# Decode attention beside a feed-forward block: K turned as 32-bit pairs, with q and P as the stationary operands

## The chip, the cores and the metric

The kernel runs on one core of one Trainium2 chip. The metric is device time in microseconds (us). The kernel before takes 122.8 us (median of 3 runs, 122.71 to 122.98).

Engine names: PE is the matrix engine (TensorE), PEld its weight loads, DVE the vector engine, ACT the scalar engine, POOL is GpSimd, SP the engine that issues the loads. A "unit" below is one batch with four KV heads: 1 MB of K and 1 MB of V. There are 16 of them.

## The reference, cut to what matters

```python
# x: [8, 1, 512]; 32 query heads, 8 KV heads of width 128; the last 1024 of 4096 cached keys are used
xn = layernorm(x)
q  = xn @ wq                                   # [512, 4096]
s  = (softmax(q k^T / sqrt(128)) v) @ wo       # over k_cache, v_cache[:, :, -1024:, :]
g  = silu((gelu(xn @ w_gate) * (xn @ w_up)) @ w_down)
return x + s * g
```

Everything is bfloat16. The work reads 47.5 MB, of which K and V are 33.6 MB (32 loads of 1,024 KB, each called 1 MB here), and produces 8 KB. The term `s * g` is so small beside `x` that an experiment that leaves attention out still passes the comparison with the reference. That comparison therefore says nothing for the experiments below that are called wrong on purpose, and little for the others: where "right result" stands below, it means that this comparison was passed by a kernel that does the whole arithmetic.

## The kernel before

All large loads go through one queue, from SP, in a fixed order: `wq`, then K and V of unit after unit, then the feed-forward weights and `wo`. A ring of ten 2 MB buffers lets the loads run ahead. One unit of attention is:

```python
def transposes(u, t):                  # four times per unit, 8 chunks of 128 (head, key) rows each
    for i in range(TG):
        nc.tensor.transpose(kT_ps[:, i*P:(i+1)*P], k_t[b][:, h, t*TG+i, :], ident)
    nc.vector.tensor_copy(out=kT, in_=kT_ps)

def scores(u, t):                      # kT is stationary, 16 columns of q move
    for i in range(TG):
        nc.tensor.matmul(sc[u][:, t*TG+i, :], kTs[u, t][:, i*P:(i+1)*P],
                         qT[:, b, h*HS:(h+1)*HS], ...)
    # after the last: ACT Exp -> pT (already with keys on partitions)

def values(u):                         # V is stationary, 16 columns of P move
    nc.tensor.matmul(sum_ps, ones_pp, pT[u], ...)
    for c in range(NCH):               # 32
        nc.tensor.matmul(oT_ps, v_t[b][:, h, c, :], pT[u][:, c, :], ...)
    nc.vector.tensor_reduce(out=sums, in_=sum_ps..., op=ALU.add)
    nc.vector.reciprocal(out=sums, in_=sums)
    nc.vector.tensor_tensor(out=oT[:, h, :, b], in0=oT_ps, in1=sums, op=ALU.mult)
# ... the loop over units issues the loads of K[u] and V[u-1], and interleaves these three
```

The projection by `wo` already uses column tiles: four matmuls with 32 stationary columns each, in four strips of the array.

The softmax here doesn't subtract the row's maximum and nothing guards it: scores larger than these inputs give would overflow.

## Time and profile before

| | before |
|---|---|
| time | 122.8 us |
| loads | 47.5 MB, DMA engines full from 3 to 112 us |
| one unit of loads | every 4.9 us |
| PE's wait for K in a unit | about 0.9 us |
| last weight lands | 116.86 us |

These are lines of the page of the kernel before. The first block gives busy time, share of the span and instructions; the strips give tenths of 40 slices of the span (9 is 90% or more), the GB/s row what the loads moved; the queue lines give packets, MB and the share of the time of 16 DMA engines; then the chain of work that ended last; then the two costliest groups (instructions, shapes, busy us, mean ns, idle time before them and its cause).

```profile
span 121.0 us, 4362 instructions
PE 85.1 (70%) x2015; PEld 78.7 (65%) x2030; DVE 69.8 (58%) x145; ACT 13.3 (11%) x22; POOL 1.4 (1%) x6
...
PEclk9999999999976999999999999599999955555555
DMA  4999999999999999999999999999999999999720
...
q1 hardware_dynamic: 5976, 47.47, 93.6%
q8 instruction: 16, 0.26, 0.8%
...
DMA 95%; DVE 0%; PE 0%; SPq 0%; issue 0%
...
L200 DVE COPY kT<-kT_ps 128x1024 bf16<-128x1024 bf16 x64 | 43.0, 692 | 16.0 <-PE kT_ps L196 16.0
L196 PE MATMUL kT_ps<-ident,k_t 128*128 128x128 bf16 x512 | 41.9, 230 | 11.8 <-DMA k_t<-in_A_k_cache_dram 11.8
```

The DMA strip is 9 from the second slice to the 37th, and the chain is DMA for 95% of the span. PE is busy for 70%, and most of what it waits for is a load (11.8 us for K, 8.4 us for `wq` at the start), which is the sign of an engine that keeps up. A note for reading on: PE's busy time is a union of overlapping, pipelined matmuls. It is not the time that PE needs per unit. The 512 transposes have a mean of 230 ns, yet eight of them take 0.61 us.

The timeline of the kernel before around one K wait (start, duration, engine, instruction, idle time and releaser):

```profile
61.79 0.46 PEld L196 LDWEIGHTS <-k_t 128*128 128x128 bf16 x8
61.81 0.61 PE L196 MATMUL kT_ps<-ident,k_t 128*128 128x128 bf16 x8
...
63.48 0.62 PE L196 MATMUL kT_ps<-ident,k_t 128*128 128x128 bf16 x8 [0.87 <-DMA k_t<-in_A_k_cache_dram]
```

### The profile page before, as it was taken

Reading aid. Unit: us, or ns where it says so; the run is one execution under the profiler, and the core shown is the slowest. Engines: PE = TensorE matmul, PEld = TensorE weight load, DVE = VectorE, ACT = ScalarE, POOL = GpSimd, SP = SyncE. Lnnn points to the kernel's source line nnn. Section 1 sums busy time; section 2 is a strip of 40 time slices with the busy share of each in tenths; the row PEclk is TensorE's granted clock in tenths of the full one; section 3 lists DMA queues with packets and bytes.
Section 4 is the critical chain, followed back from the end, with each engine's and each line's share of the span. In section 5 each row is a group of like instructions: output and inputs, shape, how many; then the busy total and the mean of one; then the engine's idle time right before and its main releaser. Section 6 shows DMA issues by size and latency. Waiting matters only on the chain.

```text
span 121.0 us, 4362 instructions
## 1 busy us (share of the span) xinstructions
PE 85.1 (70%) x2015; PEld 78.7 (65%) x2030; DVE 69.8 (58%) x145; ACT 13.3 (11%) x22; POOL 1.4 (1%) x6
## 2 busy tenths in 40 slices
PE   0000699897879978879669693997969697845760
PEld 0000699896878977769669683896968597744640
DVE  3710036886947969669687592787859400398010
ACT  4500000110101101101101010110101100100000
POOL 4000000000000000000000000000000000000000
PEclk9999999999976999999999999599999955555555
DMA  4999999999999999999999999999999999999720
GB/s 100 423 433 433 401 420 420 433 423 431 417 428 423 420 431 415 428 423 428 423 420 417 431 425 428 428 423 420 417 449 433 418 419 440 438 417 409 316 88 3
DMA packets 6009, 47.75 MB, mean 395 GB/s; under 512 B 736, under 2 KB 744, under 8 KB 1000
## 3 DMA queue, kind: packets, MB, share of 16 engines
q1 hardware_dynamic: 5976, 47.47, 93.6%
q8 instruction: 16, 0.26, 0.8%
q10 hardware_dynamic: 16, 0.01, 0.0%
q14 instruction: 1, 0.01, 0.0%
HBM read 47.46 MB, written 0.01 MB: 392 GB/s over the span
## 4 chain that ended last, share of the span: by engine, by line
DMA 95%; DVE 0%; PE 0%; SPq 0%; issue 0%
DMA k_t<-in_A_k_cache_dram 51%; DMA wg_t<-in_B_w_gate_dram 18%; DMA wo_t<-in_A_wo_dram 17%; DMA wq_t<-in_A_wq_dram 10%; PE s_ps L355 0%; SPq L89 0%; DVE tmp L363 0%; DVE out_sb L365 0%; SPq L97 0%
## 5 line engine op out<-in xcount | busy, mean ns | idle before, releaser
L200 DVE COPY kT<-kT_ps 128x1024 bf16<-128x1024 bf16 x64 | 43.0, 692 | 16.0 <-PE kT_ps L196 16.0
L196 PE MATMUL kT_ps<-ident,k_t 128*128 128x128 bf16 x512 | 41.9, 230 | 11.8 <-DMA k_t<-in_A_k_cache_dram 11.8
L196 PEld LDWEIGHTS <-k_t 128*128 128x128 bf16 x512 | 31.8, 103 | 12.9 <-DMA k_t<-in_A_k_cache_dram 12.9
L213 PE MATMUL sc_ps<-qT,kT 128*128 128x16 bf16 x512 | 22.4, 170 | 0.5 <-DVE kT L200 0.4
L213 PEld LDWEIGHTS <-kT 128*128 128x128 bf16 x512 | 20.6, 98 | 2.9 <-issue 0.8
L220 ACT ACTIVATE pT<-sc_ps 128x512 bf16<-128x512 f32 x16 | 9.6, 597 | 80.8 <-PE sc_ps L213 80.8
L231 PEld LDWEIGHTS <-v_t 128*128 128x128 bf16 x512 | 15.5, 97 | 2.4 <-issue 0.8
L231 PE MATMUL oT_ps<-pT,v_t 128*128 128x16 bf16 x512 | 15.5, 170 | 1.3 <-issue 0.5
L235 DVE TENSOR_REDUCE sums<-sum_ps 128x16 f32<-128x512 f32 x16 | 11.0, 690 | 1.4 <-PE kT_ps L196 0.7
L178 PE MATMUL qT_ps<-xnT,wq_t 128*128 128x8 bf16 x128 | 3.7, 168 | 8.4 <-DMA wq_t<-in_A_wq_dram 8.4
L178 PEld LDWEIGHTS <-wq_t 128*128 128x128 bf16 x128 | 3.6, 104 | 8.5 <-DMA wq_t<-in_A_wq_dram 8.5
L207 PE MATMUL sc_ps<-mask,ident 128*128 128x512 bf16 x15 | 6.5, 430 | 0.0
L185 DVE CAST qT<-qT_ps 128x256 bf16<-128x256 f32 x1 | 0.4, 425 | 10.2 <-PE qT_ps L178 10.2
L355 PE MATMUL s_ps<-wo_t,oR 128*32 128x128 bf16 x128 | 4.2, 309 | 2.3 <-DMA wo_t<-in_A_wo_dram 2.3
L355 PEld LDWEIGHTS <-oR 128*32 128x32 bf16 x128 | 3.4, 139 | 2.9 <-issue 2.9
L290 DVE TENSOR_SCALAR z<-z 128x112 f32<-128x112 f32 x1 | 0.2, 219 | 8.4 <-ACT z L289 8.4
L239 DVE TENSOR_TENSOR oT<-oT_ps,sums 128x16 bf16<-128x16 f32 x16 | 3.7, 229 | 2.1 <-PE kT_ps L196 0.5
L238 DVE RECIPROCAL sums<-sums 128x16 f32<-128x16 f32 x16 | 4.0, 253 | 0.5
L279 PE MATMUL gu_ps<-xnT,wg_t 128*128 128x8 bf16 x56 | 3.5, 201 | 0.8 <-DMA wg_t<-in_B_w_gate_dram 0.8
L279 PE MATMUL gu_ps<-xnT,wu_t 128*128 128x8 bf16 x56 | 3.5, 202 | 0.7 <-DMA wu_t<-in_B_w_up_dram 0.7
L279 PEld LDWEIGHTS <-wg_t 128*128 128x128 bf16 x56 | 3.4, 161 | 0.9 <-DMA wg_t<-in_B_w_gate_dram 0.9
L279 PEld LDWEIGHTS <-wu_t 128*128 128x128 bf16 x56 | 3.5, 161 | 0.8 <-DMA wu_t<-in_B_w_up_dram 0.8
(51 smaller groups left out, 26.5 us busy)
## 6 DMA issues: line engine op xcount, KB each, us to landing
k_t<-in_A_k_cache_dram SPq DMA_DIRECT2D x16, 1024.0 KB, 20.5
v_t<-in_A_v_cache_dram SPq DMA_DIRECT2D x16, 1024.0 KB, 19.8
wq_t<-in_A_wq_dram SPq DMA_DIRECT2D x2, 2048.0 KB, 9.6
wo_t<-in_A_wo_dram SPq DMA_DIRECT2D x1, 2048.0 KB, 27.6
wg_t<-in_B_w_gate_dram SPq DMA_DIRECT2D x1, 1792.0 KB, 21.6
wu_t<-in_B_w_up_dram SPq DMA_DIRECT2D x1, 1792.0 KB
wd_t<-in_B_w_down_dram SPq DMA_DIRECT2D x1, 1792.0 KB, 25.2
wo_t<-in_A_wo_dram SPq DMA_DIRECT2D x1, 1024.0 KB, 27.4
```

The lines of the kernel that those rows point to most:

```text
L178: nc.tensor.matmul(qT_ps[:, h, :], wq_t[k // 2][:, k % 2, h * Dh : (h + 1) * Dh], xnT[:, k, :], start=(k == 0), stop=(k == KD - 1),)
L196: nc.tensor.transpose(kT_ps[:, i * P : (i + 1) * P], k_t[b][:, h, t * TG + i, :], ident)
L200: nc.vector.tensor_copy(out=kT, in_=kT_ps)
L207: nc.tensor.matmul(sc[u].rearrange("p c h -> p (c h)"), ident, mask.rearrange("p c n j -> p (c n j)"), start=True, stop=False, skip_group_ ...
L213: nc.tensor.matmul(sc[u][:, t * TG + i, :], kTs[u, t][:, i * P : (i + 1) * P], qT[:, b, h * HS : (h + 1) * HS], start=False, stop=(t == NT ...
L220: nc.scalar.activation(out=pT[u], in_=sc[u], func=ACT.Exp, scale=inv_sqrt_dh)
L231: nc.tensor.matmul(oT_ps, v_t[b][:, h, c, :], pT[u][:, c, :], start=(c == 0), stop=(c == NCH - 1))
L235: nc.vector.tensor_reduce(out=sums, in_=sum_ps.rearrange("p c h -> p h c"), axis=AX.X, op=ALU.add)
L238: nc.vector.reciprocal(out=sums, in_=sums)
L239: nc.vector.tensor_tensor(out=oT[:, h, :, b], in0=oT_ps, in1=sums, op=ALU.mult)
L279: nc.tensor.matmul(gu_ps[:, w, j, :], wt[:, k, :].rearrange("p (m j) -> p j m", j=FJ)[:, j, :], xnT[:, k, :], start=(k == 0), stop=(k == K ...
L355: nc.tensor.matmul(s_ps[32 * q : 32 * (q + 1), :], oR[:, t, i, :], w[:, r, q * NW : (q + 1) * NW], start=(t == 0 and i == 0), stop=(t == N ...
```

## The change

The intent is to give PE less to do. Two neighbouring keys of 128 bf16 values are read as 128 words of 32 bits, and one fp32 transpose turns both. Then q is the stationary operand for the scores, and P for V, each with 32 columns in four column tiles, so that long rows of K and V stream through the array. P must now be turned, and partial sums of V over strips and pairs must be gathered, with fp32 matmuls against a selecting matrix that add each unit into one bank per head half. The order of units changes from batch-major to head-half-major for that gather. The diff, cut to its core:

```diff
-        b, h = divmod(u, NH)
+        h, b = divmod(u, B)
 ...
-        for i in range(TG):
-            nc.tensor.transpose(kT_ps[:, i*P:(i+1)*P], k_t[b][:, h, t*TG+i, :], ident)
+        k32 = k_t[u // 2][:, u % 2, :, :].rearrange("p c d -> p (c d)").bitcast(FP32)
+        for pc in range(NPC):                                  # 4 per group, 16 per unit
+            w = g * NPC + pc
+            nc.tensor.transpose(kT_ps[:, pc, :], k32[:, w*P:(w+1)*P], identf)
 ...
-            nc.tensor.matmul(sc[u][:, t*TG+i, :], kTs[u, t][:, i*P:(i+1)*P], qT[...], ...)
+        for r in range(2):
+            for g in range(NG):
+                nc.tensor.matmul(sc_ps[CC*g:CC*(g+1), :], Q2[:, r, b, h, :, :]...,
+                                 kTs[u, g][:, :, r], ..., tile_position=(0, CC*g))
 ...
+    def turn(u):                                               # 4 bf16 transposes of P
+        ...
+        nc.scalar.copy(out=pTs[u], in_=pT_ps)
 ...
-            nc.tensor.matmul(oT_ps, v_t[b][:, h, c, :], pT[u][:, c, :], ...)
-        nc.vector.tensor_reduce(out=sums, ...); reciprocal; product
+                nc.tensor.matmul(x_ps[CC*g:CC*(g+1), :, :]..., pTs[u][:, pc, CC*g:CC*(g+1)],
+                                 v_t[u // 2][:, u % 2, c:c+2, :]..., tile_position=(0, CC*g))
+        nc.vector.tensor_tensor(out=xs[u][:, 0:2*Dh]..., in0=x_ps, in1=own2..., op=ALU.mult)
+    def gather(u):                                             # fp32, 257 columns
+        nc.tensor.matmul(tot[h], zsel[:, B-1-b:P+B-1-b], xs[u], start=(b == 0), stop=(b == B-1))
+    def outputs(t): ...                                        # normalise, expand: once per head half
```

No byte less is read, and the loads keep their sizes, their count and their places in the queue.

## The prediction

> **What bounds the kernel now.** The DMA stream. The page's chain of work that ended last is 95% DMA; the slices show the 16 DMA engines at "9" from 3 us to about 112 us at 415 to 433 GB/s, 47.5 MB in all. The Trainium skill, "DMA: Bandwidth & Descriptors", Specifications, gives 435 GB/s as the fabric ceiling; this trace's 424 GB/s is 97% of that. The queue's own waits show loads held by earlier loads, only 0.6 us by PE releasing a buffer. One unit (1 MB of K, 1 MB of V) arrives every 4.9 us. In it PE does about 4 us of work and waits about 1 us for K (timeline, 60 to 70 us). After the last weight lands at 116.86 us there are only 12 matmuls, two DVE operations and the output DMA.
>
> **What the change does, per unit.**
> - Loads: the same sizes and counts, heads and batches in another order.
> - PE removed: 32 bf16 transposes (8 take 0.61 us, so 2.4), 32 score matmuls (1.4), 32 V matmuls (0.95), the sums matmul (0.2).
> - PE added: 16 fp32 transposes; 8 score matmuls of 512 columns and 16 V matmuls of 256 in four column tiles; 4 bf16 transposes of P; one fp32 gather of 257 columns. The old projection already has column tiles: 64 of 128 columns took 1.90 us at half clock, 30 ns each, so four overlap. Estimated from that: scores 0.45, mask 0.2, V 0.45, P 0.3, gather 0.5, tile switches 0.3: about 2.2 us besides the transposes.
> - The open term: an fp32 transpose. The skill, "TensorE: Matmul & The Clock Gate", Terms, says transpose mode is 4x faster for FP32; no instruction here shows it. At 0.08 to 0.16 us, the unit needs 3.5 to 4.8 us of PE and fits into 4.9. At 0.21 us or more (four passes, or weight load not overlapped), it needs over 5.6 and PE becomes the limit.
> - DVE: reduction, reciprocal and product go (690+253+229 ns), one 128x256 product comes (about 0.45 us); the kT copies stay (4 x 692 ns). ACT: one more copy (about 0.6 us). Neither binds.
>
> **On the critical path.** Almost nothing, if PE keeps up: saved PE time becomes longer waits for K. Prologue: constants fit into DVE's 10.2 us wait for q; the permuting of q adds about 1.5 us, absorbed by prefetch. Tail: before, the second projection half's operand is ready at 111.4 us and not needed until about 115. The new chain after the gate matmuls (end 103.9 us, half clock) is gather, P turn, ACT copy, V, DVE product, gather, normalise, expansion (1.23 us), regroup: 9 to 10 us, ready near 113.5. It still fits.
>
> **Prediction: 122.9 us, range 121.8 to 125.5; faster by over 2%: 0.03; within 2%: 0.79; slower by over 2%: 0.18.**
>
> **What would show it right.** DMA near 424 GB/s until 112 us; last weight at 116.9 us; PE busy down to 50 to 65 us with longer waits for K; DVE busy below 63 us; the chain still about 95% DMA; column-tiled matmuls starting close together.
>
> **What would make it wrong.** fp32 transposes above 0.17 us each: waits for K vanish, the DMA queue waits for PE to release slots, 127 to 135 us. Column tiles not overlapping, or slow stride-2 reads of kT: the same sign. PE at half clock in its longer waits: hurts only if a unit then exceeds 4.9 us. The tail chain running past 115 us: up to 2 us. A faster result could only come from the new address order giving DMA a better rate; I see no evidence for it.

## The result, and the profile after

The changed kernel takes 123.0 us (median of 4 runs, 122.88 to 123.15) against 122.78 us (median of the 4 runs of the kernel before that are listed with them). The ratio is 1.0016, with a 95% interval of 0.9998 to 1.0034. Ratios here and below are over runs of the same rounds, so they are not quite the ratio of the medians quoted. The same lines of the page of the changed kernel:

```profile
span 120.8 us, 2828 instructions
PE 93.8 (78%) x1214; PEld 65.2 (54%) x1214; DVE 63.2 (52%) x125; ACT 24.1 (20%) x54; POOL 1.4 (1%) x6
...
PEclk9999999999999999999999967999999965555555
DMA  3999999999999999999999999999999999999700
...
q1 hardware_dynamic: 5976, 47.47, 93.4%
q8 instruction: 9, 0.15, 0.4%
...
DMA 67%; PE 22%; DVE 4%; SPq 2%; issue 1%
...
L242 DVE COPY kT<-kT_ps 128x1024 bf16<-128x1024 bf16 x64 | 42.6, 688 | 23.1 <-PE kT_ps L240 21.8
L240 PE MATMUL kT_ps<-identf,k_t 128*128 128x128 f32 x256 | 40.4, 298 | 3.0 <-DMA k_t<-in_A_k_cache_dram 3.0
```

The DMA strip is as full as before, and the time is the same. But PE was not relieved. It executes 1,214 matmuls where there were 2,015, and yet its busy time is 93.8 us, up from 85.1. Its waits for K shrank from 11.8 to 3.0 us. The transposes' idle column moved from "waits for DMA" to almost nothing, and the chain now runs through PE for 22% of the span. If the change had freed PE, the waits for K would have grown.

Where the chain leaves the loads is visible in its list of pieces (start, duration, what):

```profile
43.74 19.48 DMA k_t<-in_A_k_cache_dram
63.36 0.64 PE kT_ps L240 x4
...
94.07 0.52 PE x_ps L283 x13
94.59 22.02 DMA wo_t<-in_A_wo_dram
```

From 63 to 94 us PE is behind the loads and catches up. It falls behind at 66 to 70 us, in the unit in which the first head half is finished: DVE normalises and expands (o_sb 0.79 us, e 1.22 us and smaller ones), with the copies of kT queued behind it, and PE stands still for 1.9 us and drops to half clock (6 and 7 in the PEclk strip). The ring of buffers absorbs it: in the queue's own waits, PE's late release of buffers costs three waits of 0.3 us, 0.9 us in all against 0.6 us in the kernel before. At 94.59 us the loads are the limit again.

### The profile page after: what moved, and what is told of

The parts are those of the page before. It is cut to its first block, busy times and chain, and to the rows that moved or that the text cites. A ratio compares the mean times of both kernels' runs of the same rounds, so it can differ in the third digit from the quotient of the medians.

```text
span 120.8 us, 2828 instructions
## 1 busy us (share of the span) xinstructions
PE 93.8 (78%) x1214; PEld 65.2 (54%) x1214; DVE 63.2 (52%) x125; ACT 24.1 (20%) x54; POOL 1.4 (1%) x6
## 4 chain that ended last, share of the span: by engine, by line
DMA 67%; PE 22%; DVE 4%; SPq 2%; issue 1%
DMA k_t<-in_A_k_cache_dram 49%; DMA wo_t<-in_A_wo_dram 18%; PE kT_ps L240 10%; PE tot L298 3%; PE sc_ps L257 3%; PE x_ps L283 3%; DVE kT L242 2%; SPq L100 2%; PE sc_ps L251 1%; PE pT_ps L274 1%; SPq L91 1%; DVE o_sb L315 1%; PE s_ps L438 0%; PE r_ps L333 0%; DVE e L322 0%
## 5 line engine op out<-in xcount | busy, mean ns | idle before, releaser
L240 PE MATMUL kT_ps<-identf,k_t 128*128 128x128 f32 x256 | 40.4, 298 | 3.0 <-DMA k_t<-in_A_k_cache_dram 3.0
L240 PEld LDWEIGHTS kT_ps<-identf,k_t 128*128 128x128 f32 x256 | 30.2, 150 | 14.1 <-issue 9.8
L266 ACT ACTIVATE p_sb<-sc_ps 128x512 bf16<-128x512 f32 x16 | 9.6, 597 | 39.6 <-PE sc_ps L257 26.0
L276 ACT COPY pT<-pT_ps 128x512 bf16<-128x512 bf16 x16 | 9.4, 586 | 31.0 <-PE pT_ps L274 31.0
L298 PE MATMUL tot<-x_u,zsel 128*128 128x257 f32 x32 | 12.2, 467 | 2.6 <-DVE x_u L289 2.4
L283 PE MATMUL x_ps<-v_t,pT 128*32 128x256 bf16 x256 | 10.4, 284 | 0.7 <-ACT pT L276 0.7
L257 PE MATMUL sc_ps<-kT,Q 128*32 128x512 bf16 x128 | 10.6, 407 | 0.0
L289 DVE TENSOR_TENSOR x_u<-x_ps,own 128x256 f32<-128x256 f32 x16 | 6.8, 422 | 2.8 <-PE x_ps L283 2.8
L251 PE MATMUL sc_ps<-maskR,maskL 128*128 128x512 bf16 x16 | 6.5, 405 | 0.0
L274 PE MATMUL pT_ps<-ident,p_sb 128*128 128x128 bf16 x64 | 6.4, 225 | 0.0
```

The lines of the kernel that those rows point to most:

```text
L240: nc.tensor.transpose(kT_ps[:, pc, :], k32[:, w * P : (w + 1) * P], identf)
L251: nc.tensor.matmul(sc_ps, maskL.rearrange("p a n j -> p (a n j)"), maskR.rearrange("p a n -> p (a n)"), start=True, stop=False, skip_group ...
L257: nc.tensor.matmul(sc_ps[CC * g : CC * (g + 1), :], Q2[:, r, b, h, :, :].rearrange("p c n -> p (c n)"), kTs[u, g][:, :, r], start=False, s ...
L266: nc.scalar.activation(out=ps[u].rearrange("p c s -> p (c s)"), in_=sc_ps, func=ACT.Exp, scale=inv_sqrt_dh, accum_out=xs[u][:, 2 * Dh : 2 ...
L274: nc.tensor.transpose(pT_ps[:, pc, :], ps[u][:, pc, :], ident)
L276: nc.scalar.copy(out=pTs[u], in_=pT_ps)
```

## The experiments

Two theories stood at the start. The first: both kernels end when the load stream ends, and PE's time per unit, which the change raised, hides under it. The rival: something the change costs and something it gains cancel (order of addresses, PE time, tail).

### The loads alone

```diff
-        transposes(u, 0)          # and all scores, values, and the gathering of outputs
 ...
     load_cache(...)               # every load of the kernel before, in its order, stays
```

> Every load of the old kernel in its order, with attention left out (the result is wrong on purpose: the attention term is zero). Theory (both kernels end when the load stream ends): within 1.2 us of the kernel before, so 121.6 to 123.5 us. Rival (both kernels sit on some common compute limit that happens to take as long): 118 us or less.

Measured: 121.25 us (121.09 to 121.35), ratio 0.9863 (0.9841 to 0.9886). The loads alone account for all but 1.65 us of the kernel before. This is a little under the expected 121.6 us, and that difference is followed up below.

### The arithmetic alone, of both kernels

```diff
-        if u > 0:
-            load_cache(A_k_cache, u, k_t, "k_t")
-            load_cache(A_v_cache, u - 1, v_t, "v_t")
+        if u == 1:
+            load_cache(A_v_cache, 0, v_t, "v_t")
 ...      # every unit reads the K and V of unit 0
```

> The old kernel's arithmetic in full, but K and V of one unit are loaded and used for all 16 (wrong on purpose). What is left is the compute limit. Theory: about 4.0 us per unit in the middle, 92 to 100 us in all, far under 122.8. Rival (compute binds as well): above 115 us.

> The same for the changed kernel (wrong on purpose). Theory (PE time per unit went up from about 4.0 to about 4.33 us, and hides under the loads): 4 to 7 us longer than the same test of the old kernel, and still under 108 us. Rival (the change saves PE time, as the prediction had it, and the saving is hidden): 3 us or more shorter than that test.

Measured: 103.16 us for the kernel before (expected 92 to 100; my allowance for the ends was too small), and 113.54 us for the changed one. Both are under the loads, but the changed kernel needs 10.4 us more, not 4 to 7, was not under the 108 us expected, and leaves only some 9 us to the load-bound time. Had the change freed PE, it would have been shorter.

The timelines show what one unit costs. First the arithmetic alone of the kernel before, DVE over one unit:

```profile
63.36 2.64 DVE L200 COPY kT<-kT_ps 128x1024 bf16<-128x1024 bf16 x4
...
65.94 0.69 DVE L235 TENSOR_REDUCE sums<-sum_ps 128x16 f32<-128x512 f32 x1
...
66.66 0.25 DVE L238 RECIPROCAL sums<-sums 128x16 f32<-128x16 f32 x1
...
67.02 0.23 DVE L239 TENSOR_TENSOR oT<-oT_ps,sums 128x16 bf16<-128x16 f32 x1
67.19 2.63 DVE L200 COPY kT<-kT_ps 128x1024 bf16<-128x1024 bf16 x4
```

DVE has no gap worth naming: 63.36 to 67.19 is 3.83 us per unit. PE has none either: over six such units (42.97 to 65.94 us) DVE is busy for 22.14 and PE for 22.55 of 22.97 us. So both are full at 3.83 us, and this run does not tell which of the two sets it. Then the arithmetic alone of the changed kernel, PE over one unit:

```profile
70.55 1.04 PE L240 MATMUL kT_ps<-identf,k_t 128*128 128x128 f32 x8
71.43 0.38 PE L251 MATMUL sc_ps<-maskR,maskL 128*128 128x512 bf16 x1
71.74 0.63 PE L257 MATMUL sc_ps<-kT,Q 128*32 128x512 bf16 x8
72.30 0.66 PE L240 MATMUL kT_ps<-identf,k_t 128*128 128x128 f32 x4
72.89 0.62 PE L283 MATMUL x_ps<-v_t,pT 128*32 128x256 bf16 x16
73.44 0.66 PE L240 MATMUL kT_ps<-identf,k_t 128*128 128x128 f32 x4
74.11 0.70 PE L298 MATMUL tot<-x_u,zsel 128*128 128x257 f32 x2
74.65 0.39 PE L274 MATMUL pT_ps<-ident,p_sb 128*128 128x128 bf16 x4
74.88 1.04 PE L240 MATMUL kT_ps<-identf,k_t 128*128 128x128 f32 x8
```

Read the starts, not the durations, since matmuls overlap. From 70.55 to 74.88 is 4.33 us per unit. PE is the limit, and DVE, which lost its reduction, waits. So the change moved the limit of the arithmetic from DVE and PE alike at 3.83 us to PE alone at 4.33 us. Both lie under the 4.9 us in which a unit arrives. Spare time per unit went from about 1.07 us to about 0.57 us, which goes with PE's waits for K in the two full kernels (0.87 us in the line shown before; in the changed kernel 0.34 to 0.46 us in six of seven waits, 0.69 us in the other).

The 10.4 us are not fully accounted for: 16 x 0.50 us is 8.0 us, and the stall in the unit that finishes the first head half adds about 3.8 us (the two units there take 6.63 and 5.87 us instead of 4.33 each). The sum is 1.4 us too much. What the changed kernel gains at its ends was not measured.

### The order of units alone

```diff
-        b, h = divmod(u, NH)
+        h, b = divmod(u, B)       # in the kernel before; slots follow u // 2
```

> The old kernel with nothing but the changed kernel's order of heads and batches. Theory: the order of addresses does nothing, ratio 0.997 to 1.003. Rival (the order costs or gains time and the rest of the change hides it): outside of 0.995 to 1.005.

Measured: 122.97 us, ratio 1.0006 (0.9987 to 1.0024). The new order of addresses does nothing. The rival of two cancelling effects loses its first candidate.

### The 1.65 us between the loads and the whole kernel

The DMA strips of both kernels and of the loads alone are equally full to about 112 us. They differ in the last few us. The last load gives each of the 16 DMA engines eight packets of 3 KB, and each engine closes its share with a packet of 4 bytes. From the traces' lists of DMA packets, these are the ends of the engines (us from the span's start):

```
loads alone  14 engines from 113.3 to 113.7, 2 at 115.1
before       7 engines from 113.4 to 113.8, 2 from 114.5 to 114.9, 7 from 116.1 to 116.6
changed      15 engines up to 115.0, 1 at 116.2
```

The engines do not finish together, and the output waits for the last. The profile's queue 8, which it calls "instruction", moved 16 packets of 16 KB in the kernel before (`q8` in the page lines above), 9 in the changed kernel, and 3 in the loads alone. The Trainium skill, "Runtime: NRT & Kernel Launch", Instruction fetch mechanics, says that a sequencer fetches its own instructions in blocks of 16 KiB, which are 256 instructions, through a DMA queue, and that this is "mostly hidden". The traces agree on the size, and nearly on the count: the kernel before has 4,045 recorded PE instructions and 16 fetches, 253 for each.

In the kernel before the fetches lie mostly 6 to 8.5 us apart, each takes about 0.9 us, and a load packet of 8 KB that would take about 310 ns is found at about 0.8 us soon after most of them. The sum is steady: the fetches at 18.58, 44.90 and 57.52 us took 928, 879 and 941 ns, the packets that began as they ended took 813, 856 and 800 ns instead of 309, so each pair took 1.43 us more than the packet alone. All 11 such pairs in this trace and all seven in that of the changed kernel give 1.42 to 1.43 us. So a second theory: the fetches take time from single DMA engines, and the most delayed engine ends the kernel. Two runs tell it from the rival that PE's activity slows the loads. Each adds dummy work of about equal PE busy time to the loads alone:

```diff
+    for i in range(1300):                                  # many small
+        nc.tensor.transpose(dummy_ps, ident, ident)
```

```diff
+    for i in range(330):                                   # few large
+        nc.tensor.matmul(dummy_ps, ident, mask_512_columns, start=True, stop=True)
```

> The loads-only kernel with 1,300 dummy 128-column transposes (2,600 PE instructions that read and write nothing the kernel needs) after q. Theory (the 16 KB instruction fetches, one per about 256 PE instructions, share the DMA engines with the loads, and the load stream ends when the most delayed engine ends): about 10 fetches more than the 3 of loads-only, last weight landing 0.8 to 1.6 us later, so 122.0 to 123.0 us. Rival (what separates loads-only from the kernel before is something else): 121.3 us as loads-only.

> The control: about the same PE busy time in 330 dummy matmuls of 512 columns (660 instructions). Theory (instruction fetches): about 2 or 3 fetches more than loads-only, 121.3 to 121.8 us, at least 0.5 us under the run with many small ones. Rival (PE activity as such slows the loads): as long as the run with many small ones.

From the pages of the loads alone with many small and with few large dummies:

```profile
span 120.8 us, 3593 instructions
PE 91.3 (76%) x1728; PEld 89.9 (74%) x1728; DVE 6.4 (5%) x27; ACT 3.7 (3%) x6; POOL 1.4 (1%) x6
...
q8 instruction: 13, 0.21, 0.6%
```

```profile
span 119.4 us, 1646 instructions
PE 89.9 (75%) x751; PEld 48.2 (40%) x758; DVE 6.4 (5%) x27; ACT 3.7 (3%) x6; POOL 1.4 (1%) x6
...
q8 instruction: 6, 0.10, 0.3%
```

Measured: 122.44 us with many small (ratio 0.9962, 0.9947 to 0.9978) and 121.0 us with few large (0.9848, 0.9834 to 0.9861), which is no longer than the loads alone and a little under the expected 121.3. PE is equally busy in both, so its busy time is not what slows the loads. Weight loads differ as well (89.9 against 48.2 us), so the pair alone does not prove the fetches.

The changed kernel has seven fetches fewer, and most of its engines do finish earlier. But one, at 116.2 us, spoils it: the last weight lands at 116.66 us, only 0.20 us earlier than before (one profile of each, and the profiled run of the kernel before was a slow one of its kind, 123.09 us). Two packets that begin as the fetch of 114.3 us ends, or just after, take 334 ns instead of 121. It was tempting to believe that this one late fetch eats the gain.

```diff
+    for i in range(72):           # in the wait for the first weights; moves the later fetches
+        nc.tensor.transpose(dummy_ps, ident, ident)
```

> The changed kernel, right result, with 72 dummy transposes in the wait for the first weights, which move the last instruction fetch (114.3 us in the profile, beside the last load) to an earlier place. Theory (that fetch delays the one engine that ends last, 116.2 us where all others have ended by 115.0): last weight lands 0.8 to 1.4 us earlier, 121.6 to 122.4 us, ratio to the kernel before 0.990 to 0.996. Rival (the fetch costs the same wherever it lies): 123.0 us, ratio 1.000 to 1.003.

Measured: 123.17 us, ratio 1.0021 (1.0009 to 1.0034). The theory about that one late fetch falls. The ninth fetch moved to 111.0 us as intended (a tenth came at 115.4 us), no packet of the last load was stretched any more, and one engine still ended at 116.48 us.

So not where the ninth fetch lies, but that there is a ninth? The ends of the engines in all runs up to then fall into three groups, near 113.4, 114.8 and 116.3 us. With 5 fetches before 114.5 us, 5 engines were in the middle group; with 12, four were in the middle and four in the last. That is what one gets if each fetch delays its engine by about 1.4 us and fetches go round 8 of the 16 engines. The fetches' own durations say the same: in the kernel before the first eight took 928, 966, 960, 949, 879, 881, 941 and 931 ns, and the next seven 922, 960, 962, 949, 879, 879 and 941 ns, a pattern that repeats after eight. Then the first eight fetches cost the kernel one delay, and the ninth to sixteenth a second one. Two runs were made on this:

```diff
+    for i in range(788):          # the loads alone, aimed at 8 fetches before the end
+        nc.tensor.transpose(dummy_ps, ident, ident)
```

> The loads-only kernel with 788 dummy transposes, chosen so that 8 instruction fetches come before the last load ends (one more at about 115 us). In the runs so far the engines' ends of the last load fall into groups at about 113.4, 114.8 and 116.3 us, and their sizes agree with each fetch delaying its engine by about 1.4 us and fetches going round 8 of the 16 engines: 5 fetches, 5 engines in the second group; 12 fetches, 4 in the second and 4 in the third. Theory (that): 8 engines near 114.8 us, none near 116.3, time 120.9 to 121.3 us as with 6 fetches. Rival (the delay grows evenly with the number of fetches): some engine near 115.5 us or later, 121.4 to 121.7 us.

Measured: 122.51 us, ratio 0.9971 (0.9954 to 0.9987). The run missed its aim: the ninth fetch came at 114.2 us, before the end of the last load, so it has nine. It shows what the theory says of nine: one engine ends at 116.36 us, and no other after 115.1. It also shows that the delay does not grow evenly, since 9 fetches cost as much as the 12 of the run with many small dummies (122.51 and 122.44 us).

```diff
     # in the changed kernel: q = xn @ wq with xn stationary (32 columns) in four column tiles
-    for h in range(Hq):
-        for k in range(KD):
-            nc.tensor.matmul(qT_ps[:, h, :], wq_t[k//2][:, k%2, h*Dh:(h+1)*Dh], xnT[:, k, :], ...)
+    for k in range(KD):
+        for t in range(2):
+            for q in range(4):
+                j = 4 * t + q
+                nc.tensor.matmul(q_ps[t][32*q:32*(q+1), :], xnT32[:, k, :],
+                                 wq_t[k//2][:, k%2, j*512:(j+1)*512], ..., tile_position=(0, 32*q))
+    # two copies to bf16, then 8 transposes of 128x128, each of four heads, and two copies to qT
```

> The changed kernel with the projection of q done with x stationary in four column tiles and 8 transposes, 40 matmuls instead of 128: the same numbers, 176 PE instructions fewer, so that the fetch at 114.3 us (the ninth, the second on its engine by the theory above) is not made before the last load ends. Theory: no engine ends the last load after 115.2 us, the last weight lands near 115.4 instead of 116.7 us, 121.5 to 122.0 us, ratio to the kernel before 0.988 to 0.994. Rival (the engine that ends last is late for another reason): 122.8 to 123.1 us.

From its page, and the last matmuls on the last weights in the timelines of the kernel before, of the changed kernel and of this one, in this order:

```profile
span 119.7 us, 2657 instructions
...
q8 instruction: 9, 0.15, 0.4%
```

```profile
116.90 0.51 PE L355 MATMUL s_ps<-wo_t,oR 128*32 128x128 bf16 x12 [0.21 <-DMA wo_t<-in_A_wo_dram]
```

```profile
116.66 0.51 PE L438 MATMUL s_ps<-wo_t,oR 128*32 128x128 bf16 x12 [1.53 <-DMA wo_t<-in_A_wo_dram]
```

```profile
115.67 0.51 PE L455 MATMUL s_ps<-wo_t,oR 128*32 128x128 bf16 x12 [0.20 <-DMA wo_t<-in_A_wo_dram]
```

Measured: 121.83 us (121.69 to 121.89), ratio 0.9913 (0.9898 to 0.9927), a right result by the comparison on the chip (no check on record would notice an error in attention). This version is 0.9% faster than the kernel before, clear of the noise. It still makes nine fetches, but the ninth comes at 116.2 us, after the last load. No engine ends later than 115.3 us, and the last weights are used 1 us earlier. Over all runs with the full loads, with the fetches counted up to 114.5 us, the time by which every engine without such a delay has ended:

| run | fetches before 114.5 us | engines ending after 115.5 us | last engine ends, us |
|---|---|---|---|
| loads alone | 3 | 0 | 115.1 |
| loads, few large dummies | 5 | 0 | 115.0 |
| changed, q in column tiles | 8 | 0 | 115.3 |
| changed | 9 | 1 | 116.2 |
| loads, 788 dummies | 9 | 1 | 116.4 |
| changed, transposes twice | 9 | 1 | 116.3 |
| changed, fetch moved | 9 | 1 | 116.5 |
| loads, many small dummies | 12 | 4 | 116.4 |
| before, in the new order | 15 | 7 | 116.5 |
| before | 15 | 7 | 116.6 |

The step lies between 8 and 9 fetches, and the third column is the number of fetches beyond 8 in every row. The step and the counts show that in these runs the number of fetches before the end decides when the loads end. (The number of PE instructions goes with the number of fetches; it is the stretched packets beside the fetches that point to the fetches.) Later fetches are left out of the count: in the run with many small dummies a thirteenth began at 115.0 us and in the one with the fetch moved a tenth at 115.4 us, before the last engine ended, and neither added a late engine. By the theory their own engines had ended by then. (In the loads alone the third fetch, at 113.6 us, came when most engines had ended.) That fetches go round eight engines is inferred from these counts and from the durations that repeat after eight; the records do not name the engine of a fetch.

### What the fp32 gather and the stall cost

```diff
-    zsel = ...FP32;  xs[u] = ...FP32
+    zsel = ...BF16;  xs[u] = ...BF16        # in the arithmetic alone of the changed kernel
```

> The compute-only test of the changed kernel with the partial sums and the selecting matrix in bf16 (wrong and coarser on purpose), so the gather is one pass. Theory (the fp32 gather is the largest mis-sized term, 0.70 us and a wait of about 0.25 us per unit): 4.33 us per unit falls to about 3.9, 113.5 us to 105 to 108. Rival (the transposes and the tile switches set the 4.33 us): above 110 us.

Measured in one look: 105.91 us, against 113.54. In its timeline a unit takes 3.89 us (start of the gather to start of the next, 69.63, 73.53, 77.41), so the fp32 form of the gather costs about 0.44 us in each unit. As a term of the prediction's sum the gather was not too small (0.5 us forecast, 0.54 us between the starts above). But the fp32 form alone turns a change that would have left PE about as DVE had been (3.83) into one that leaves it slower.

```diff
-        nc.vector.tensor_tensor(out=e, ...)                             # first head half
+        nc.gpsimd.tensor_tensor(out=e, ...)                             # and regroup(0) one unit later
```

> The compute-only test of the changed kernel with the first head half's 128x2048 expansion on GpSimd and its regrouping one unit later. Theory (in unit 10 the normalising and expanding stand before the kT copies on DVE, PE idles and falls to half clock, about 3.8 us in all): 109 to 112 us against 113.5, and no half clock near 61 to 68 us. Rival (that stall costs nothing): 113.5 us.

Measured in one look: 111.47 us against 113.54, and no half clock in that unit. Taking the 1.2 us expansion off DVE's queue returns about 2 us of the stall estimated at 3.8 us (the four runs of the test without it lie between 112.61 and 113.89 us, so one look leaves 1.1 to 2.4); the other DVE work of that unit still stands before the copies (PE's wait at the gather is 0.57 us instead of 1.92).

### How near the edge is

```diff
-        for pc in range(NPC):
+        for pc in list(range(NPC)) * 2:     # each fp32 transpose of K twice, right result
```

> The changed kernel, right result, with each fp32 transpose of K done twice into the same place: as if one took about 0.22 us, the case that the prediction called the break point. Theory (PE has about 0.6 us per unit to spare under the loads, no more): a unit takes 4.33 + 16 x 0.11 = 6.1 us, PE becomes the limit, 134 to 142 us. Rival (PE time is hidden far beyond that, because PE was never near binding): under 125 us.

```profile
span 133.4 us, 3326 instructions
...
PE 79%; DMA 9%; DVE 6%; issue 2%; ACT 0%; SPq 0%; ACTq 0%
```

Measured: 135.53 us, ratio 1.1035 (1.0993 to 1.1077). A unit in the middle takes 5.79 us (gather starts at 55.46, 61.25, 67.04, 72.83; 6.1 expected), and the chain is PE for 79%. The prediction's condition was real: the change was about 0.6 us per unit away from the point where PE becomes the limit, and 1.46 us more per unit cost 10%.

The version with q in column tiles (121.83 us) is the fastest complete kernel. The loads with few instructions, at 121.0 to 121.3 us, show that at most another 0.7% or so is to be had without reading fewer bytes or ordering them otherwise.

## Why the prediction was right or wrong

- **The time: right.** 122.9 us was forecast with "within 2%", 123.0 us was measured. The reason given, that the load stream bounds both kernels, is shown by the loads alone (121.25 us), by both arithmetic-alone runs under 122 us (103.16 and 113.54), and by the unchanged DMA strip. The prediction's range for a unit, 3.5 to 4.8 us of PE for a transpose of 0.08 to 0.16 us, holds the measured 4.33 us. How close the number came is partly luck: the loads end as late as before only because a ninth fetch, which the prediction did not count, comes before their end. With eight, 121.83 us was measured, still just inside the range.
- **The fp32 transpose: right.** The estimate was 0.08 to 0.16 us. Eight follow each other in 0.88 us, so 0.11 us each, against 0.057 us for a bf16 one (0.46 us of weight loads for eight). The skill, "TensorE: Matmul & The Clock Gate", Terms, speaks of a transpose mode that is 4x faster for FP32; no run here has an fp32 transpose outside that mode to compare, so the factor is not shown, only that 0.11 us is well under the 0.21 us that the prediction called the break point. But a pair turned as words costs as much as two chunks turned singly (16 x 0.11 = 1.76 us against 32 x 0.057 = 1.82 us), so this part of the change gains PE almost nothing.
- **"Saved PE time becomes longer waits for K", "PE busy down to 50 to 65 us": wrong.** PE busy rose to 93.8 us and its waits for K fell from 11.8 to 3.0 us. The step that failed is the saving itself. The work that the prediction lists as removed sums to 4.95 us, but the whole old unit takes 3.83 us: it added durations of overlapping instructions (0.61 us for eight transposes; in the run of the arithmetic alone the next group starts 0.45 us after their start, so 32 cost 1.8 us and not 2.4). The new side was under-counted too, in "about 2.2 us besides the transposes": with 0.11 us for a transpose that sum gives 3.96 us; 4.33 was measured. Even 3.96 us would have saved nothing. Against the estimates, from the starts in the timeline above: transposes with tile switches 2.14 us (1.76 + 0.3), mask and scores 0.87 (0.65), V 0.55 (0.45), gather 0.54 (0.5), turning P 0.23 (0.3). No term is far off; nearly all are a little too small. Nor was it seen that DVE was as full as PE in the old arithmetic.
- **DVE below 63 us: a near miss.** 63.2 us. The reduction went, as forecast, and DVE is no longer near a limit.
- **Prologue and tail: right.** The gates end at 102.4 us and the second half's operand is ready at about 111.4 us (forecast 113.5), before the last weights. The last weight landed at 116.66 us (forecast 116.9).
- **The chain "still about 95% DMA": wrong.** It is 67%, because PE fell behind at 66 to 70 us and caught up by 94 us. The stall behind DVE's normalising was not foreseen. No cost of it is seen in the end: the ring covered it, and the last weight landed no later.
- **"A faster result could only come from the new address order": wrong, though it did not show.** The order does nothing (ratio 1.0006). The change removed seven instruction fetches, which the prediction did not think of as load on the DMA engines. It removed one too few: with nine before the end there is still one doubly delayed engine, and with eight the same kernel takes 121.83 us.
- **"What would make it wrong": confirmed.** Doing each transpose twice (about 0.2 us for both) gave 135.53 us. The forecast for such a case was 127 to 135, so a little low.

## What to carry to other kernels

When the loads fill the whole span, compare the time per arriving piece (here 4.9 us) with the time between starts of the same instruction in consecutive pieces, not with busy time; a change below that line buys nothing, and may quietly spend the slack, as this one did (1.07 to 0.57 us), since longer rows, wider words and an fp32 gather can take back all that fewer instructions save. To see such a hidden loss, run the arithmetic without the loads and the loads without the arithmetic. If the loads are the limit, look at when each DMA engine ends its share of the last load, and count the instruction fetches that share the engines.

## What the Trainium skill lacked or had wrong

- "Runtime: NRT & Kernel Launch", Instruction fetch mechanics, calls the cost of crossing a 16 KiB block "mostly hidden", and does not say that the fetches take time from the DMA engines of the kernel's loads. In a kernel bound by its loads that is not hidden: one fetch delays one engine by about 1.4 us, and the last load ends at 115.0 to 115.3 us with up to 8 fetches before 114.5 us, and at 116.2 to 116.6 us with 9 to 15. No page has the step at 8.
- "TensorE: Matmul & The Clock Gate", Part 4, says that full clock does not engage for transposes. In the run with 1,300 dummy transposes the granted clock was 1.00 from 20 to 90 us, with nothing but bf16 transposes on PE, 57 ns apart (74.5 us for 1,300). Whether these run in the page's transpose mode the profile does not say.
- "TensorE: Matmul & The Clock Gate", Terms, has "4x faster for FP32" but no duration of an fp32 transpose. Here a 128x128 one repeats every 0.11 us, twice the bf16 time.
